# Layer 3: when VectorE normalises and turns the last row tile

## The chip, the cores and the metric

The kernel runs on one core of one Trainium2 chip. The metric is the time of one execution in device microseconds (us). Five engines work side by side, each with its own queue that it runs in order: TensorE (PE; its weight loads are shown as PEld), VectorE (DVE), ScalarE (ACT), GpSimd (POOL) and SyncE (SP), which issues the transfers between the chip's memory (DRAM) and the on-chip memory. Engines wait for one another only where an instruction needs what another has written, or a buffer that another still reads.

## The reference

Four layers run over 2048 rows of 576 numbers: attention, MLP, attention, MLP, each on the layer-normalised rows, each with a residual sum. The attention is linear, with 32 heads of 18.

```python
def _A_ref(x, wqkv, wo):
    B, S, D = x.shape
    H = 32; Dh = D // H
    qkv = (x @ wqkv).reshape(B, S, 3, H, Dh).transpose(2, 0, 3, 1, 4)
    q, k, v = qkv[0], qkv[1], qkv[2]
    phi = lambda t: jnp.where(t > 0, t + 1, jnp.exp(t)) + 1e-6
    pq, pk = phi(q), phi(k)
    kv = jnp.einsum("bhsd,bhse->bhde", pk, v)
    z = jnp.einsum("bhsd->bhd", pk)
    num = jnp.einsum("bhqd,bhde->bhqe", pq, kv)
    den = jnp.einsum("bhqd,bhd->bhq", pq, z)[..., None] + 1e-6
    o = num / den
    return o.transpose(0, 2, 1, 3).reshape(B, S, D) @ wo

x = A_x
x = x + _A_ref(_layernorm(x), A_wqkv, A_wo)
x = x + _B_ref(_layernorm(x), B_w1, B_b1, B_w2, B_b2)   # gelu MLP, 576 -> 4608 -> 576
x = x + _A_ref(_layernorm(x), A_wqkv, A_wo)
x = x + _B_ref(_layernorm(x), B_w1, B_b1, B_w2, B_b2)
```

## The kernel before

**Tiles and names.** The 2048 rows are cut into 16 row tiles t = 0 to 15 of 128 rows, and into 4 blocks c of four tiles. In the code the layers are numbered `li` = 0 to 3, so the third layer is `li` = 2 and of kind "A". `yT` holds the normalised rows turned, with the 576 features along the partitions in five chunks of 128, and the 2048 rows along the free dimension: it is what the projections of queries and keys read.

**From a layer's sum to the next layer's turned rows.** A small state machine (`LNPipe`, from line 342) takes each row tile through the layer norm, one stage per tick: statistics on VectorE (lines 392 to 410), the reciprocal root as a power on GpSimd (line 428), the normalisation into one of three `y_ring` buffers (line 465, on VectorE for the tiles that concern us), and for layer 3 a store of the normalised rows to memory (line 472). One stage later `turn_rows` (line 294) turns 32 x 32 squares of the tile with a VectorE instruction into `turned` (line 297). With the fourth tile of a block, four stores put the turned block into memory (line 305). Three ticks on, `land` loads the block back into its columns of `yT` (lines 320 and 323). For the last block, block 3, it then also loads the last columns of the normalised rows into `v_ring` (line 328) and the rows of tiles 12 to 15 into `yrow_pair` (line 290).

**The last tile.** Tile 15's sum at the end of layer 2 ends that layer's matmuls, so its layer norm runs while layer 3 has already begun. Its statistics carry an order behind a key or query maximum (the `after="phi"` of line 1088, read at line 394); its normalisation and its turning carry none but the data. The places of all instructions on an engine are settled when the program is built, by a scheduler that follows the program's order and such order-only dependencies (`add_manual_dep` with `NOSYNC`).

**The key loop of layer 3** (lines 851 to 862). Step t issues, on TensorE, ten key matmuls in two halves of five (`k_half`, line 645), five query matmuls for one group of heads and one block of 512 rows (`q_proj`, line 614), and five products of the keys and rows of step t - 1 (`rows_by_keys`, line 670). The block 3 of `yT` is read first by the key matmuls of step 12. Each key half and each query tile goes through phi: ScalarE takes the exponential (lines 530 and 547) and, for the first key half and the queries, the value plus one (line 548); VectorE takes a minimum (lines 532 and 553) and a maximum (lines 534 and 555). The second key half takes the value straight from PSUM at line 534, so its PSUM buffer is free only after that maximum. The PSUM pool for these tiles has four buffers, one of which is held throughout the loop by `k2_tail`; the other three go around, so the second key half of step t + 1 needs the buffer of the second key half of step t. `dve_last["phi"]` names the latest maximum issued so far.

**Ticks.** The loop ticks the state machine once per step from step 4 on and a second time from step 7 on. Tile 15 gets its statistics with step 4's tick, its power with step 5's, its normalisation with step 6's and its turning with step 7's first.

**After the loop** come the sums over keys for the other half, the denominators, the output projection with its residual sums (line 598), whose residual rows are loaded at line 574, and layer 4.

Of the kernel before, what the change touches and what calls it, by code (L numbers as in the profile page):

```python
# [16 lines left out]
NT = S // P  # L17
# [17 lines left out]
def build(tc, A_x, A_wqkv, A_wo, B_w1, B_b1, B_w2, B_b2, out, dbg=None, n_layers=4):  # L35
    nc = tc.nc
    dbg = dbg or {}
    with ExitStack() as ctx:
# [112 lines left out]
        NOSYNC = mybir.DependencyInfo(mybir.DependencyClass.NoSync, mybir.DependencyReason.SCHED_ONLY)  # L151
# [22 lines left out]
        def named(name, inst):  # L174
            first_ones[name] = inst
            return inst
# [82 lines left out]
        dve_last = dict(norm=None, sum=None, phi=None)  # L259
# [12 lines left out]
        def first_tail(t, width=65):  # L272

            slot = 2 * (t % 8) + t // 8
            flat = v_ring[slot // 8][:].rearrange("p g c -> p (g c)")
            return flat[:, (slot % 8) * 65:(slot % 8) * 65 + width]
# [17 lines left out]
        def turn_rows(y, t, kind):  # L294

            c, j = divmod(t, TPC)
            turn = nc.vector.transpose(out=turned[:, :, j, :], in_=y[:, 0:D])
            if dve_last["sum"] is not None:
                tc.add_manual_dep(turn.ins, dve_last["sum"], NOSYNC, reason="rows are turned behind the sums")
            if j < TPC - 1:  # L300
                return
            home = y_d[state["turns"] % 2]
            state["turns"] += 1
            for i in range(4):
                store = nc.sync.dma_start(out=home[:, :, i * P:(i + 1) * P].rearrange("j r n -> r j n"),
                                          in_=turned[32 * i:32 * (i + 1), :, :, :].rearrange("r j t c -> r j (t c)"))
            landing.append([3, home, c, kind])
            if kind == "A" and c == NCB - 1:
                sp_last["turned"] = store.ins.name
# [32 lines left out]
        class LNPipe:  # L342
# [11 lines left out]
            def tick(self, transposes=1):  # L354
                land()
                for it in list(self.items):
# [32 lines left out]
                    elif st == 0:  # L389
                        xt = it["xt"]  # L390
                        stt = work.tile([P, 2, 6], F32, name="ln_st", bufs=4)
                        first = nc.vector.bn_stats(out=stt[:, 0, :], in_=xt[:, 0:HALF])
                        second = nc.vector.bn_stats(out=stt[:, 1, :], in_=xt[:, HALF:D])
                        after = dve_last[it["after"]] if it["after"] in ("sum", "phi") else it["after"]
# [34 lines left out]
                    elif st == 2 and it["norm"] != "dve":  # L429
                        nmr = work.tile([P, 1], F32, name="ln_nmr", bufs=4)  # L430
                        nc.gpsimd.tensor_scalar(out=nmr[:], in0=it["mv"][:, 0:1], scalar1=1.0 if it["stats"] == "act" else -1.0,
                                                scalar2=it["rstd"][:, 0:1], op0=ALU.mult, op1=ALU.mult)
                        it["nmr"] = nmr
                    elif st in (2, 3) and it["kind"] == "A" and it["evac"] == "act":
                        xt, t = it["xt"], it["t"]
                        tail = first_tail(t)[:, 0:64]
                        if it["norm"] == "pool":
                            for out, cols in ((xt[:, 0:4 * P], slice(0, 4 * P)), (tail, slice(4 * P, D))):
                                norm = nc.gpsimd.tensor_scalar(out=out, in0=xt[:, cols], scalar1=it["rstd"][:, 0:1],
                                                               scalar2=it["nmr"][:, 0:1], op0=ALU.mult, op1=ALU.add)  # L440
                            pool_last["norm"] = norm.ins.name
                        else:
                            for name, out, cols in ((f"n{t}", xt[:, 0:4 * P], slice(0, 4 * P)), (f"nt{t}", tail, slice(4 * P, D))):
                                norm = named(name, nc.vector.tensor_scalar(
                                    out=out, in0=xt[:, cols], scalar1=it["mv"][:, 0:1], scalar2=it["rstd"][:, 0:1],
                                    op0=ALU.subtract, op1=ALU.mult))
                            dve_last["norm"] = norm.ins.name
                        row_of[t] = xt
                        it["stage"] = 4
                        continue  # L450
                    elif st in (2, 3):
                        if sum(other["stage"] == 4 for other in self.items) == NY:
                            continue
                        y = y_ring[state["ycnt"] % NY]
                        state["ycnt"] += 1
                        xt = it["xt"]
                        if it["norm"] == "act":
                            nc.scalar.activation(out=y[:, 0:D], in_=xt[:, 0:D], func=ACT.Identity,
                                                 scale=it["rstd"][:, 0:1], bias=it["nmr"][:, 0:1])
                        elif it["norm"] == "pool":  # L460
                            norm = nc.gpsimd.tensor_scalar(out=y[:, 0:D], in0=xt[:, 0:D], scalar1=it["rstd"][:, 0:1],
                                                           scalar2=it["nmr"][:, 0:1], op0=ALU.mult, op1=ALU.add)
                            pool_last["norm"] = norm.ins.name
                        else:
                            norm = nc.vector.tensor_scalar(out=y[:, 0:D], in0=xt[:, 0:D], scalar1=it["mv"][:, 0:1],
                                                           scalar2=it["rstd"][:, 0:1], op0=ALU.subtract, op1=ALU.mult)
                            dve_last["norm"] = norm.ins.name
                        if it["kind"] == "B" and it["evac"] != "dma":
                            nc.gpsimd.tensor_copy(out=y[:, D:DPAD], in_=y[:, 4 * P:D])
                        if it["kind"] == "A" and it["evac"] == "dma":  # L470
                            c, j = divmod(it["t"], TPC)
                            nc.sync.dma_start(out=yrow_d[c, :, j], in_=y[:, 0:D])
                        it["y"] = y
                        it["stage"] = 4
                        continue
                    elif st == 4:
                        t = it["t"]
                        first_layer = it["kind"] == "A" and it["evac"] == "act"
                        y = it["xt"] if first_layer else it["y"]
                        if it["evac"] == "dma":  # L480
                            turn_rows(y, t, it["kind"])
                            self.items.remove(it)
                            continue
                        tp = ps_h.tile([P, 512], F32, name="tp", tag="h")
                        tp = tp[:, 0:DPAD // 2].bitcast(BF16).rearrange("p (k n) -> p k n", k=KD)
                        first = first_layer and t < 2
                        tp2 = tp
                        if first:
                            tp2 = ps_h.tile([P, 512], F32, name="tp2", tag="h")
                            tp2 = tp2[:, 0:DPAD // 2].bitcast(BF16).rearrange("p (k n) -> p k n", k=KD)  # L490
                        for k in range(KD):
                            block = first_tail(t, P) if first_layer and k == 4 else y[:, k * P:(k + 1) * P]
                            pe(nc.tensor.transpose(out=(tp if k < 3 else tp2)[:, k, :], in_=block, identity=ident[:]))  # L493
                        if first:
                            named(f"ca{t}", nc.scalar.copy(out=yT[:, 0:3, t * P:(t + 1) * P], in_=tp[:, 0:3, :]))
                            named(f"cd{t}", nc.vector.tensor_copy(out=yT[:, 3:KD, t * P:(t + 1) * P], in_=tp2[:, 3:KD, :]))
                        elif it["evac"] == "act":
                            turned_tile = nc.scalar.copy(out=yT[:, :, t * P:(t + 1) * P], in_=tp)
                            act_last["turned"] = turned_tile.ins.name
                            if first_layer and t < 5:  # L500
                                named(f"ca{t}", turned_tile)
                            elif act_last["exp"] is not None:
                                tc.add_manual_dep(turned_tile.ins, act_last["exp"], NOSYNC, reason="keys go on first")
                        else:
                            nc.vector.tensor_copy(out=yT[:, :, t * P:(t + 1) * P], in_=tp)
                        self.items.remove(it)
                        continue
# [678 lines left out]
```

## Time and profile before

| | |
|---|---|
| median of 3 runs | 762.07 us (761.74 to 762.75) |
| the profiled execution | 762.17 us |
| its span, first to last instruction | 760.5 us |
| granted TensorE clock | 1.000 |
| TensorE busy | 753.6 us |
| VectorE busy | 270.5 us |
| ScalarE busy | 327.9 us |
| GpSimd busy | 117.4 us |

How to read the profile: times are in us from the span's start unless marked ns. A row of the order of time has start, duration, engine, line, operation, tiles as out<-in, shapes and a count; what stands in brackets is the idle time of that engine ahead of the instruction and what ended it. A row of waits has the waiting engine and line, what released it, the total, the number of times and the longest. In the chain that ended last each row has start, duration and what the end waited for in that time. Instructions overlap a little on an engine, so the start of the next one, not the duration, tells how long an instruction holds its queue. The ends of matmuls are modelled.

### The profile page before, as it was taken

The numbers are of one execution on the slowest core, as the hardware profiler recorded it, in microseconds if no ns is written. First come the engines' busy times: TensorE is split into PE (matmuls) and PEld (weight loads), VectorE is DVE, ScalarE is ACT, GpSimd is POOL, SyncE is SP. The second block draws the span as 40 slices with busy tenths as digits, with TensorE's granted clock in tenths as the row PEclk, the third lists the DMA queues.
The fourth block names the chain that finished last, engine by engine and source line by source line (L and its number), as shares of the span: only waits on it lengthen the run. The fifth ranks groups of instructions, "written<-read, shape, count | busy, mean of one in ns | idle before, by whom it ended". The sixth has DMA issues, their size and how long they took to land.

```text
span 760.5 us, 15743 instructions
## 1 busy us (share of the span) xinstructions
PE 753.6 (99%) x6563; PEld 489.4 (64%) x6563; DVE 270.5 (36%) x685; ACT 327.9 (43%) x729; POOL 117.4 (15%) x194
## 2 busy tenths in 40 slices
PE   8999999999999999999999999999999999999998
PEld 5777754774477457646777777447645754674476
DVE  8876862136033503401357577600230132000000
ACT  5886656205700650263056566660164036205600
POOL 4840241002000301200100005300020020001000
PEclk9999999999999999999999999999999999999999
DMA  8994573026312711320304047530240033011000
GB/s 235 266 320 62 169 269 82 17 64 190 82 40 83 179 51 48 112 65 28 120 24 118 18 137 248 191 83 16 79 115 15 16 125 83 9 32 56 1 10 22
DMA packets 80897, 73.82 MB, mean 97 GB/s; under 512 B 36730, under 2 KB 65466, under 8 KB 80826
## 3 DMA queue, kind: packets, MB, share of 16 engines
q1 hardware_dynamic: 80826, 72.82, 32.9%
q8 instruction: 51, 0.84, 0.4%
q14 instruction: 20, 0.16, 0.1%
HBM read 48.03 MB, written 24.77 MB: 96 GB/s over the span
## 4 chain that ended last, share of the span: by engine, by line
PE 95%; DVE 1%; POOL 1%; ACT 1%; DMA 1%; SPq 0%; issue 0%; POOLq 0%; DVEq 0%
PE m_ps L1077 36%; PE h_ps L1019 20%; PE hp_ps L1019 16%; PE q_ps L614 6%; PE k_ps L645 4%; PE wo_ps L907 4%; PE k_ps L670 4%; PE m_half L1077 1%; PE k_tail L670 1%; PE tp L493 1%; DMA x<-in_A_x_dram 1%; PE kv_ps L695 0%; ACT turned L788 0%; PE rden_ps L784 0%; PE den_ps L743 0%
## 5 line engine op out<-in xcount | busy, mean ns | idle before, releaser
L1077 PE MATMUL m_ps<-w_sb,hT 128*128 128x288 bf16 x2232 | 274.8, 286 | 0.0
L1077 PEld LDWEIGHTS <-hT 128*128 128x128 bf16 x2304 | 224.8, 98 | 59.8 <-issue 3.4
L1019 PEld LDWEIGHTS <-w_sb 64*128 64x128 bf16 x2304 | 124.5, 94 | 136.5 <-issue 1.9
L1019 PE MATMUL hp_ps<-yT,w_sb 64*128 64x512 bf16 x1152 | 178.0, 376 | 0.0
L1019 PE MATMUL h_ps<-yT,w_sb 64*128 64x512 bf16 x1152 | 147.9, 376 | 0.0
L1024 ACT COPY relay_sb<-relay_sb 128x1 f32<-128x1 f32 x144 | 28.7, 199 | 259.8 <-PE h_ps L1019 217.5
L1015 ACT ACTIVATE hT<-h_ps,b1T 128x512 bf16<-128x512 f32 x144 | 91.2, 685 | 44.3 <-PE h_ps L1019 44.3
L428 POOL TENSOR_TENSOR ln_rstd<-ln_u,neg_half 128x1 f32<-128x1 f32 x61 | 35.0, 576 | 444.5 <-DVE ln_u L410 219.5
L1015 ACT ACTIVATE hT<-hp_ps,b1T 128x512 bf16<-128x512 f32 x144 | 91.3, 693 | 0.0
L598 DVE TENSOR_TENSOR xbf<-m_ps,xo 128x576 bf16<-128x576 f32 x15 | 11.4, 758 | 213.6 <-PE m_ps L1077 213.6
L598 DVE TENSOR_TENSOR xo<-m_ps,xo 128x576 f32<-128x576 f32 x16 | 12.1, 758 | 174.9 <-PE m_ps L1077 174.9
L581 POOL TENSOR_TENSOR xo<-xo,b_bc 128x576 f32<-128x576 f32 x32 | 41.1, 1288 | 100.8 <-DMA xo<-x_d 62.9
L1019 PE MATMUL h_ps<-yT,w_tail 64*128 64x512 bf16 x144 | 54.1, 376 | 0.0
L1019 PE MATMUL hp_ps<-yT,w_tail 64*128 64x512 bf16 x144 | 54.1, 376 | 0.0
L614 PE MATMUL q_ps<-yT,wqkv_sb 128*126 128x512 bf16 (+1 forms) x200 | 49.3, 379 | 0.1
L645 PE MATMUL k_ps<-wqkv_sb,yT 128*128 128x288 bf16 x320 | 44.8, 286 | 0.9 <-DVE pk L534 0.8
L907 PE MATMUL wo_ps<-kvwo,pq 126*128 126x288 bf16 (+1 forms) x320 | 43.3, 286 | 0.2
L1019 PEld LDWEIGHTS <-w_tail 64*128 64x128 bf16 x288 | 27.1, 94 | 17.1
L645 PEld LDWEIGHTS <-yT 128*128 128x128 bf16 x320 | 31.0, 98 | 9.7 <-issue 1.0
L907 PEld LDWEIGHTS <-pq 126*128 126x128 bf16 (+1 forms) x320 | 30.3, 97 | 8.8 <-issue 0.6
L614 PEld LDWEIGHTS <-wqkv_sb 128*126 128x126 bf16 (+1 forms) x200 | 25.7, 131 | 11.7 <-issue 0.5
L547 ACT ACTIVATE phi_e<-q_ps 126x512 bf16<-126x512 f32 (+1 forms) x40 | 24.0, 599 | 18.4 <-PE q_ps L614 16.7
(131 smaller groups left out, 592.3 us busy)
## 6 DMA issues: line engine op xcount, KB each, us to landing
xo<-x_d SPq DMA_DIRECT2D x48, 288.0 KB, 3.6
x_d<-xo SPq DMA_DIRECT2D x32, 288.0 KB, 2.6
xl<-x_d SPq DMA_DIRECT2D x24, 288.0 KB, 4.3
y_d<-turned SPq DMA_DIRECT2D x40, 144.0 KB, 3.4
w_sb<-in_B_w_dram SPq DMA_DIRECT2D x6, 864.0 KB, 11.0
yT<-y_d SPq DMA_DIRECT2D x10, 512.0 KB, 4.4
w_sb<-in_B_w_dram SPq DMA_DIRECT2D x9, 512.0 KB, 7.7
x_d<-xn SPq DMA_DIRECT2D x16, 288.0 KB, 3.5
```

What stands on the lines that cost most here:

```text
L428: nc.gpsimd.tensor_tensor(out=rstd[:], in0=it["u"][:], in1=neg_half[:], op=ALU.pow)
L547: exp = nc.scalar.activation(out=e_out, in_=ps_ap, func=ACT.Exp)
L581: nc.gpsimd.tensor_tensor(out=xo[:], in0=xo[:], in1=b2_bc[:], op=ALU.add)
L598: total = nc.vector.tensor_tensor(out=xn[:, cols].rearrange("p (h n) -> p h n", h=2), in0=halves, in1=xo[:, cols].rearrange("p (h n) -> p ...
L614: pe(nc.tensor.matmul(qp[0:GR[g], :], lhsT=wqkv_sb[:, k, GO[g]:GO[g] + GR[g]], rhs=yT[:, k, c * CA:(c + 1) * CA], start=(k == 0), stop=(k ...
L645: pe(nc.tensor.matmul(kp[:, 0:HALF], lhsT=yT[:, k, t * P:(t + 1) * P], rhs=wqkv_sb[:, k, D + half * HALF: D + (half + 1) * HALF], start=(k ...
L670: pe(nc.tensor.matmul(dst, lhsT=lhsT, rhs=pk, start=(t == 0), stop=(t == NT - 1)))
L907: pe(nc.tensor.matmul(wp[:, half, 0:HALF], lhsT=pq[(g, c)][0:GR[g], j * P:(j + 1) * P], rhs=kvwo[g][0:GR[g], half * HALF:(half + 1) * HALF ...
L1015: act_last["gelu"] = nc.scalar.activation(out=to, in_=ps, func=ACT.Gelu_apprx_tanh, bias=b1T[:, f:f + 1], scale=1.0).ins.name
L1019: mm = pe(nc.tensor.matmul(dst[n], lhsT=wt, rhs=mv, start=(seen[n] == 0), stop=(seen[n] == 8)))
L1024: relay = nc.scalar.copy(out=relay_sb[:, 1:2], in_=relay_sb[:, 0:1])
L1077: pe(nc.tensor.matmul(acc[half][:, 0:HALF], lhsT=hT[f][:, j * P:(j + 1) * P], rhs=w2_sb[:, f, half * HALF:(half + 1) * HALF], start=(f == ...
```

## The change

Two order-only dependencies are added; no instruction is added, removed or altered. In `turn_rows`, the turning of tile 15 in a layer of kind "A" is put behind the latest maximum issued so far. In the state machine, the normalisation of an item with `after="phi"`, which only tile 15 of layer 2's end has, is put behind the latest maximum too.

```diff
@@ -297,6 +297,8 @@
             turn = nc.vector.transpose(out=turned[:, :, j, :], in_=y[:, 0:D])
             if dve_last["sum"] is not None:
                 tc.add_manual_dep(turn.ins, dve_last["sum"], NOSYNC, reason="rows are turned behind the sums")
+            if kind == "A" and t == NT - 1:
+                tc.add_manual_dep(turn.ins, dve_last["phi"], NOSYNC, reason="keys go on first")
             if j < TPC - 1:
                 return
             home = y_d[state["turns"] % 2]
@@ -464,6 +466,8 @@
                         else:
                             norm = nc.vector.tensor_scalar(out=y[:, 0:D], in0=xt[:, 0:D], scalar1=it["mv"][:, 0:1],
                                                            scalar2=it["rstd"][:, 0:1], op0=ALU.subtract, op1=ALU.mult)
+                            if it["after"] == "phi":
+                                tc.add_manual_dep(norm.ins, dve_last["phi"], NOSYNC, reason="keys go on first")
                             dve_last["norm"] = norm.ins.name
                         if it["kind"] == "B" and it["evac"] != "dma":
                             nc.gpsimd.tensor_copy(out=y[:, D:DPAD], in_=y[:, 4 * P:D])
```

On VectorE the queue around it changes as follows (in the program's order, with the step in brackets): before, key minimum [4], normalisation, key maximum [4], query minimum [4], turning, query maximum [4], then the keys and the query of steps 5, 6 and on. After, the keys and queries of steps 4 and 5 stand first, then the normalisation, then those of step 6, then the turning, then those of step 7. The other engines' instructions keep their order.

## The prediction, made before the changed kernel ran

> **What bounds the kernel now.** I read the page first: TensorE (PE) is busy for nearly the whole span, so only an edit that changes when TensorE stands still can move the time.
>
> ```profile
> span 760.5 us, 15743 instructions
> PE 753.6 (99%) x6563; PEld 489.4 (64%) x6563; DVE 270.5 (36%) x685; ACT 327.9 (43%) x729; POOL 117.4 (15%) x194
> ```
>
> Then I read TensorE's waits from the start of layer 3 (382 us) to the end. There are two, and the larger is the one that the change is about: TensorE waits for `pk`, a key tile that VectorE writes.
>
> ```profile
> PE k_ps L645 <- DVE pk L534: 0.8, 1, 0.8
> PE tp L493 <- POOL y_ring L469: 0.4, 1, 0.4
> ```
>
> The chain that ended last shows what made `pk` late: the normalisation of row tile 15 (line 465) on VectorE, then the key maximum (line 534). Behind it in the chain come the key matmuls of step 5.
>
> ```profile
> 398.19 0.86 DVE y_ring L465
> 399.05 0.37 DVE pk L534
> ```
>
> TensorE's order of time gives the size. A step t of the key loop is ten key matmuls, five query matmuls and the products of the step before. Rows: start, duration, engine.
>
> ```profile
> 394.98 1.39 PE L645 MATMUL k_ps<-wqkv_sb,yT 128*128 128x288 bf16 x10
> ...
> 397.90 0.78 PE L645 MATMUL k_ps<-wqkv_sb,yT 128*128 128x288 bf16 x5
> 399.46 0.77 PE L645 MATMUL k_ps<-wqkv_sb,yT 128*128 128x288 bf16 x5 [0.79 <-DVE pk L534]
> 400.07 1.24 PE L614 MATMUL q_ps<-yT,wqkv_sb 128*126 128x512 bf16 x5
> ...
> 401.76 1.39 PE L645 MATMUL k_ps<-wqkv_sb,yT 128*128 128x288 bf16 x10
> 404.68 1.39 PE L645 MATMUL k_ps<-wqkv_sb,yT 128*128 128x288 bf16 x10
> 407.60 1.39 PE L645 MATMUL k_ps<-wqkv_sb,yT 128*128 128x288 bf16 x10
> 419.26 1.39 PE L645 MATMUL k_ps<-wqkv_sb,yT 128*128 128x288 bf16 x10
> ```
>
> These are steps 4, 5 (in two parts), 6, 7, 8 and 12. Steps 6 to 12 take (419.26 - 401.76) / 6 = 2.92 us each, step 4 takes 397.90 - 394.98 = 2.92, and step 5 takes 401.76 - 397.90 = 3.86. So the stall costs 0.94 us, more than the 0.79 in brackets, which starts only at the modelled end of the matmul before. A second way agrees: five key matmuls advance TensorE by 400.07 - 399.46 = 0.61, so the second half was due at 397.90 + 0.61 = 398.51 and began 0.95 late.
>
> **The change part by part.** No instruction is added or removed. On VectorE two move; TensorE, ScalarE, GpSimd and SyncE keep their order. The two have these neighbours now:
>
> ```profile
> 395.69 0.42 DVE L555 TENSOR_TENSOR pq<-phi_a,phi_e 126x512 bf16<-126x512 bf16 x1 [0.19 <-ACT phi_a L548]
> 396.03 0.45 DVE L392 BATCH_NORM_STATS2 ln_st<-xo 128x6 f32<-128x288 f32 x1
> ...
> 397.37 0.23 DVE L532 TENSOR_SCALAR phi_e<-phi_e 128x288 bf16<-128x288 bf16 x1
> 398.19 0.86 DVE L465 TENSOR_SCALAR y_ring<-xo,ln_mv,ln_rstd 128x576 bf16<-128x576 f32 x1 [0.59 <-POOL ln_rstd L428]
> 398.97 0.44 DVE L534 SCALAR_TENSOR_TENSOR pk<-k_ps,phi_e 128x288 bf16<-128x288 f32 x1
> ...
> 399.58 0.76 DVE L297 STREAM_TRANSPOSE turned<-y_ring 128x576 bf16<-128x576 bf16 x1
> 400.27 0.37 DVE L555 TENSOR_TENSOR pq<-phi_a,phi_e 72x512 bf16<-72x512 bf16 x1
> ...
> 402.52 0.43 DVE L555 TENSOR_TENSOR pq<-phi_a,phi_e 126x512 bf16<-126x512 bf16 x1 [0.25 <-ACT phi_a L548]
> 403.02 0.23 DVE L553 TENSOR_SCALAR phi_e<-phi_e 128x288 bf16<-128x288 bf16 x1
> ...
> 403.63 0.23 DVE L532 TENSOR_SCALAR phi_e<-phi_e 128x288 bf16<-128x288 bf16 x1
> 403.90 0.46 DVE L534 SCALAR_TENSOR_TENSOR pk<-k_ps,phi_e 128x288 bf16<-128x288 f32 x1
> 404.90 0.29 DVE L553 TENSOR_SCALAR phi_e<-phi_e 126x512 bf16<-126x512 bf16 x1 [0.54 <-ACT phi_e L547]
> 405.38 0.43 DVE L555 TENSOR_TENSOR pq<-phi_a,phi_e 126x512 bf16<-126x512 bf16 x1 [0.19 <-ACT phi_a L548]
> 405.94 0.24 DVE L553 TENSOR_SCALAR phi_e<-phi_e 128x288 bf16<-128x288 bf16 x1
> ```
>
> The normalisation goes from in front of the key maximum of step 4 (398.97) to behind the query maximum of step 5 (402.52); the turning goes from in front of the query maximum of step 4 (400.27) to behind that of step 6 (405.38).
>
> *What is taken away.* Without line 465 in between, the key maximum follows its minimum as at 403.63 and 403.90, 0.27 later: 397.37 + 0.27 = 397.64, done at 398.10. TensorE wants it at 398.51. The stall goes with 0.41 us to spare: -0.94 us.
>
> *What the normalisation costs in its new place.* All times behind step 5 come 0.94 earlier, so the query maximum of step 5 starts at 401.58. The next instruction follows such a maximum after 0.34 (395.69 to 396.03): the normalisation starts at 401.92, its inputs long ready, and holds the queue for 398.97 - 398.19 = 0.78, to 402.70. The gap behind the maximum is otherwise 0.56 (405.38 to 405.94), so the next key minimum is late by 0.34 + 0.78 - 0.56 = 0.56. Queued behind it are the key maxima of step 6; the second comes 403.90 - 403.02 = 0.88 after that minimum, at 403.58, done at 404.04. Who waits for it is step 7's second half, due at 404.68 - 0.94 + 0.61 = 404.35. Margin 0.31, cost nothing; VectorE's wait of 0.54 at 404.90 absorbs the delay. Without that cover the price would be at most the whole 0.78.
>
> *The turning* is the same sum: behind the maximum at 405.38 - 0.94 = 404.44 it starts at 404.78 and holds the queue for 400.27 - 399.58 = 0.69. The key minimum behind is late by 0.34 + 0.69 - 0.56 = 0.47, the second key maximum comes at 404.78 + 0.69 + 0.88 = 406.35, done at 406.81, and step 8's second half is due at 407.60 - 0.94 + 0.61 = 407.27. Margin 0.46, cost nothing; at most 0.69.
>
> *What hangs on the two.* SyncE's queue is in order. The store of the normalised rows (line 472) waits for the first, and behind it stand the stores that wait for the second:
>
> ```profile
> 400.37 2.84 SPq L305 DMA_DIRECT2D y_d<-turned  x4
> 405.88 0.38 SPq L320 DMA_DIRECT2D yT<-y_d  x1
> 406.31 0.51 SPq L323 DMA_DIRECT2D yT<-y_d  x1
> 406.92 0.53 SPq L328 DMA_DIRECT2D v_ring<-yrow_d  x1
> 407.50 1.92 SPq L290 DMA_DIRECT2D yrow_pair<-yrow_d  x4
> 409.46 0.43 SPq L574 DMA_DIRECT2D xo<-x_d  x1
> ```
>
> All of them move with the turning, by 404.78 - 399.58 = 5.20 us. The times from issue to landing, for lines 305, 320 and 323 (minimum, median, maximum over the run) and for line 290 in this stretch:
>
> ```profile
> DMA to landing us min/median/max: 2.3/3.4/4.4
> ```
> ```profile
> DMA to landing us min/median/max: 4.2/4.4/5.4
> ```
> ```profile
> DMA to landing us min/median/max: 4.0/4.6/5.3
> ```
> ```profile
> yrow_pair<-yrow_d SPq DMA_DIRECT2D x4, 128.0 KB, 3.5
> ```
>
> The turned rows of tiles 12 to 15 then land at 405.88 + 5.20 + 4.4 = 415.5 and 406.31 + 5.20 + 4.6 = 416.1. Step 12 is the first to read them, at 419.26 - 0.94 = 418.3. Of a slack of 419.26 - 410.9 = 8.4 us now, 2.2 is left. With the longest store (4.4 for 3.4) and the longest load (5.4 for 4.4, 5.3 for 4.6) it is still 0.5. The row loads of line 290 land by 409.4 + 5.2 + 3.5 = 418.1 and are read in step 13, one step after 418.3; line 328 is as small a load and stands ahead of them; the residual row of line 574 waits for the sums behind the loop. Cost nothing.
>
> *What follows.* All later work is released by TensorE, and so shifts whole by 0.94. The only other outside clock would be a transfer, and those are issued behind work that shifts too.
>
> **The sum**, against the profiled execution (762.17 us, of which 760.5 is span): 762.17 - 0.94 + 0 + 0 + 0 = 761.23. That execution stands 0.10 above the median of 762.07, so the median would go to about 761.1; I take 761.2.
>
> One rule bears on the slack. These stores are made of short pieces: in the stretch from 398 to 405.9 us,
>
> ```profile
> DMA packets 2501, 0.75 MB, mean 94 GB/s; under 512 B 2372, under 2 KB 2500, under 8 KB 2500
> ```
>
> The Trainium skill, page "DMA: Bandwidth & Descriptors", section Specifications, says that transfers below 512 B miss line rate, because the engine reads and rewrites. That speaks against handing over these rows late; its cost lies within the 3.4 us already counted, so the sum stays as it is. Only if a second such stream ran at the same time would, as an estimate of mine, the stores take 3.4 us more, 1.2 beyond the slack, and the sum be 762.4.
>
> **The rivals.** (1) *The stall moves one or two steps on.* The margins of 0.31 and 0.46 are smaller than the one removed. For it: VectorE's order is strict, and a signal later than I count by 0.3 us eats the first. Against it: the query minimum at 404.90 waits 0.54 for ScalarE, and that idle time lies where the instructions go. With no margin at all both cost their whole hold: 761.23 + 0.78 + 0.69 = 762.7; with one margin missed by half its hold, 761.6.
>
> (2) *The gain is given back later*, so the change doesn't bring what the stall cost. For it: the end of layer 3 has a chain through GpSimd (the 0.4 us wait above) and two waits for residual rows. Against it:
>
> ```profile
> DVE xo L598 <- DMA xo<-x_d: 1.2, 2, 0.6
> ```
>
> these are waits for loads that are issued behind stores that themselves shift. It gives 762.2.
>
> (3) *Slower: the turned rows come too late for step 12.* Place: the key matmuls at 418.3; price: one for one beyond the slack of 2.2. For it: it is a store to memory and a load back, both 5.20 us later, and three quarters of the slack goes. Against it: the longest landings still leave 0.5. To be slower by 0.2% they must come 2.2 + 0.94 + 1.5 = 4.6 us later than counted; if both hops take twice their median (3.4 and 4.6 more), TensorE waits 8.0 - 2.2 = 5.8 and the time is 767.0.
>
> **How the numbers follow.** What a measurement of this kernel can tell from no change is 0.2%, 1.52 us: 760.55 to 763.59. Forecast 0.72, with 760.5 to 761.8 as its own range (the three runs shown lie from 0.33 below to 0.68 above their median); of this 0.11 falls below 760.55, by the spread alone. Rival 1 0.09, rival 2 0.10, both within 0.2%; rival 3 0.09, mostly above 763.59. So faster 0.11, same 0.80, slower 0.09. The range reaches over rivals 1 and 2 at most of their prices, 760.4 to 762.5.
>
> **What would show it.** In the changed profile: TensorE's waits from 382 us on without `pk`; steps 5, 6 and 7 all at 2.92 us; the normalisation at about 401.9 with no wait for GpSimd ahead of it, the turning at 404.8; the load of line 320 issued near 411.1, and step 12 starting near 418.3 without a wait for `yT`. The forecast is wrong if step 7 or 8 is longer than 2.92 (rival 1), if step 13 starts 0.94 early and the next layer doesn't (rival 2), or if TensorE waits for a transfer at step 12 (rival 3).

## The result, and the profile after

| | kernel before | changed kernel |
|---|---|---|
| median of 21 runs each | 762.05 us (761.45 to 762.81) | 760.74 us (760.51 to 761.26) |
| the profiled execution | 762.17 us | 761.09 us |
| its span | 760.5 us | 759.4 us |

The ratio is 0.9986, with a 95% interval from 0.9979 to 0.9992: the changed kernel is faster by 0.14%, 1.3 us, and the interval goes from 0.6 to 1.6 us. That is inside the 0.2% called "no change" in the prediction, inside its range, and close to its 761.2.

The page of the changed kernel shows the same work in a shorter span, and TensorE's waits from 382 us on have lost the row for `pk`; one wait is left:

```profile
span 759.4 us, 15742 instructions
PE 753.7 (99%) x6563; PEld 489.5 (64%) x6563; DVE 270.3 (36%) x685; ACT 327.6 (43%) x729; POOL 117.3 (15%) x194
```
```profile
PE tp L497 <- POOL y_ring L473: 0.4, 1, 0.4
```

(Lines of the changed kernel are 2 or 4 higher: 465 is 467 now, 534 is 538, 645 is 649, 320 is 322.) TensorE's order of time for steps 4, 5, 6, 7, 8 and 12, each row the ten key matmuls of a step:

```profile
394.85 1.39 PE L649 MATMUL k_ps<-wqkv_sb,yT 128*128 128x288 bf16 x10
...
397.77 1.39 PE L649 MATMUL k_ps<-wqkv_sb,yT 128*128 128x288 bf16 x10
...
400.68 1.39 PE L649 MATMUL k_ps<-wqkv_sb,yT 128*128 128x288 bf16 x10
...
403.60 1.39 PE L649 MATMUL k_ps<-wqkv_sb,yT 128*128 128x288 bf16 x10
...
406.52 1.39 PE L649 MATMUL k_ps<-wqkv_sb,yT 128*128 128x288 bf16 x10
...
418.18 1.39 PE L649 MATMUL k_ps<-wqkv_sb,yT 128*128 128x288 bf16 x10
```

Step 5 is whole again, one row in place of two, and takes 400.68 - 397.77 = 2.91 us; steps 6 and 7 take 2.92 each. Steps 4 and 5 together took 401.76 - 394.98 = 6.78 before and take 400.68 - 394.85 = 5.83 now: 0.95 us. Step 12 starts when TensorE comes to it. VectorE's order of time shows the two in their new places:

```profile
397.24 0.22 DVE L536 TENSOR_SCALAR phi_e<-phi_e 128x288 bf16<-128x288 bf16 x1
397.50 0.46 DVE L538 SCALAR_TENSOR_TENSOR pk<-k_ps,phi_e 128x288 bf16<-128x288 f32 x1
...
401.44 0.43 DVE L559 TENSOR_TENSOR pq<-phi_a,phi_e 126x512 bf16<-126x512 bf16 x1 [0.25 <-ACT phi_a L552]
401.79 0.57 DVE L467 TENSOR_SCALAR y_ring<-xo,ln_mv,ln_rstd 128x576 bf16<-128x576 f32 x1
402.27 0.23 DVE L557 TENSOR_SCALAR phi_e<-phi_e 128x288 bf16<-128x288 bf16 x1
...
403.10 0.46 DVE L538 SCALAR_TENSOR_TENSOR pk<-k_ps,phi_e 128x288 bf16<-128x288 f32 x1
...
404.57 0.42 DVE L559 TENSOR_TENSOR pq<-phi_a,phi_e 126x512 bf16<-126x512 bf16 x1 [0.46 <-ACT phi_a L552]
404.91 0.77 DVE L297 STREAM_TRANSPOSE turned<-y_ring 128x576 bf16<-128x576 bf16 x1
405.61 0.19 DVE L557 TENSOR_SCALAR phi_e<-phi_e 128x288 bf16<-128x288 bf16 x1
...
406.39 0.46 DVE L538 SCALAR_TENSOR_TENSOR pk<-k_ps,phi_e 128x288 bf16<-128x288 f32 x1
```

The key maximum of step 4 follows its minimum by 0.26. The normalisation starts at 401.79 without a wait, and lasts 0.57 where it lasted 0.86 before. SyncE issues the stores and loads of the turned rows so much later:

```profile
405.71 2.46 SPq L307 DMA_DIRECT2D y_d<-turned  x4
410.94 0.38 SPq L322 DMA_DIRECT2D yT<-y_d  x1
411.37 0.51 SPq L325 DMA_DIRECT2D yT<-y_d  x1
```

### The profile page after: what moved, and what is told of

It is laid out like the page before. It is cut to its first block, busy times and chain, and to the rows that moved or that the text cites. A ratio compares the mean times of both kernels' runs of the same rounds, so it can differ in the third digit from the quotient of the medians.

```text
span 759.4 us, 15742 instructions
## 1 busy us (share of the span) xinstructions
PE 753.7 (99%) x6563; PEld 489.5 (64%) x6563; DVE 270.3 (36%) x685; ACT 327.6 (43%) x729; POOL 117.3 (15%) x194
## 4 chain that ended last, share of the span: by engine, by line
PE 97%; POOL 1%; ACT 1%; DVE 1%; issue 0%; POOLq 0%
PE m_ps L1081 36%; PE h_ps L1023 21%; PE hp_ps L1023 16%; PE q_ps L618 6%; PE k_ps L649 5%; PE k_ps L674 4%; PE wo_ps L911 4%; PE m_half L1081 1%; PE k_tail L674 1%; PE tp L497 1%; PE warm_ps L214 1%; PE kv_ps L699 0%; ACT turned L792 0%; PE rden_ps L788 0%; PE den_ps L747 0%; PE kvwo_half L717 0%
```

## The experiments

Two questions stood open: whether the normalisation's place alone made the stall, or both moves share the gain; and how much slack for the turned rows is left. The traces raised a third: why the normalisation was shorter in its new place.

**Each move alone.** In the first kernel the turning's new dependency is taken out of the changed kernel, in the second the normalisation's.

```diff
-            if kind == "A" and t == NT - 1:
-                tc.add_manual_dep(turn.ins, dve_last["phi"], NOSYNC, reason="keys go on first")
...
-                            if it["after"] == "phi":
-                                tc.add_manual_dep(norm.ins, dve_last["phi"], NOSYNC, reason="keys go on first")
```

Expected of the first: 

> Only the normalisation's order is kept; the turning is free again and stands one place behind it, between two key instructions of step 6. Theory (the stall is the place of the normalisation, 0.94 us): no wait of TensorE for pk, step 5 takes 2.92 us, and the time is that of the changed kernel, 760.7. Rival (both moves share the gain): step 5 about 3.4 us and about 761.4.

Expected of the second: 

> Only the turning's order is kept; the normalisation stands where it stood before. Theory: the wait for pk stays at 0.8 us, step 5 takes 3.86 us, and the time is that of the kernel before, 762.0. Rival (both moves share the gain): about 761.4.

Measured: the normalisation alone gives 760.68 us, 0.9984 of before (0.9975 to 0.9993), the whole gain. The turning alone gives 761.94 us, 0.9999 (0.9990 to 1.0007): nothing. TensorE's steps 5 and 6 with the normalisation alone, 400.41 - 397.50 = 2.91 us apart:

```profile
397.50 1.39 PE L647 MATMUL k_ps<-wqkv_sb,yT 128*128 128x288 bf16 x10
...
400.41 1.39 PE L647 MATMUL k_ps<-wqkv_sb,yT 128*128 128x288 bf16 x10
```

The turning reads the normalised rows, so it can't stay where it was; without a dependency of its own it stands just behind the normalisation, with one key minimum in between:

```profile
402.15 0.77 DVE L297 STREAM_TRANSPOSE turned<-y_ring 128x576 bf16<-128x576 bf16 x1
```

And with the turning alone, first TensorE's step 5 in its two parts and step 6, then the two VectorE rows that matter:

```profile
397.48 0.78 PE L647 MATMUL k_ps<-wqkv_sb,yT 128*128 128x288 bf16 x5
399.50 0.77 PE L647 MATMUL k_ps<-wqkv_sb,yT 128*128 128x288 bf16 x5 [1.24 <-DVE pk L536]
...
401.80 1.39 PE L647 MATMUL k_ps<-wqkv_sb,yT 128*128 128x288 bf16 x10
```
```profile
397.77 1.32 DVE L467 TENSOR_SCALAR y_ring<-xo,ln_mv,ln_rstd 128x576 bf16<-128x576 f32 x1 [0.59 <-POOL ln_rstd L430]
399.01 0.44 DVE L536 SCALAR_TENSOR_TENSOR pk<-k_ps,phi_e 128x288 bf16<-128x288 f32 x1
```

So the gain hangs on the normalisation's place: the later turning without it brings nothing, and the turning's own dependency adds nothing to it. But step 5 takes 401.80 - 397.48 = 4.32 here, an excess of 1.40 and not 0.94, because the normalisation, in the same place behind the same wait, lasted 1.32 and not 0.86.

**One place later is not enough.** The third kernel puts the normalisation directly behind the key maximum that it stood in front of, the least move that frees that maximum. `phi_by_dve` keeps a list of its maxima, and the last but one, when the normalisation is issued, is that of step 4. The turning's dependency is taken out. Against the changed kernel (the line that makes the empty list is left out here):

```diff
             dve_last["phi"] = top.ins.name
+            maxima.append(top.ins.name)
...
                             if it["after"] == "phi":
-                                tc.add_manual_dep(norm.ins, dve_last["phi"], NOSYNC, reason="keys go on first")
+                                tc.add_manual_dep(norm.ins, maxima[-2], NOSYNC, reason="keys go on first")
...
-            if kind == "A" and t == NT - 1:
-                tc.add_manual_dep(turn.ins, dve_last["phi"], NOSYNC, reason="keys go on first")
```

Expected: 

> The normalisation is put just one place later, right behind the key maximum of step 4, and the turning stays two places behind it as before. Theory: step 5 takes 2.92 us, but the second key maximum of step 6's predecessor now ends at about 401.48 on the clock of before, against 401.43 when step 6's second half is due, so a stall of about 0.1 us appears in step 6: 760.85. Rival 1 of the prediction (the stall moves on): half of it or more comes back in step 6, 761.3 or slower.

(The sentence says "the second key maximum of step 6's predecessor": that of step 5.) Measured: 761.47 us, 0.9992 of before (0.9983 to 1.0000), 0.7 us above the changed kernel. Step 5 has its 2.92 us, and a stall opens in step 6. TensorE's steps 6 (in two parts) and 7, then VectorE's query minimum of step 4, the turning behind it and the second key maximum of step 5:

```profile
400.28 0.78 PE L650 MATMUL k_ps<-wqkv_sb,yT 128*128 128x288 bf16 x5
401.36 0.77 PE L650 MATMUL k_ps<-wqkv_sb,yT 128*128 128x288 bf16 x5 [0.30 <-DVE pk L538]
...
403.66 1.39 PE L650 MATMUL k_ps<-wqkv_sb,yT 128*128 128x288 bf16 x10
```
```profile
398.43 0.69 DVE L558 TENSOR_SCALAR phi_e<-phi_e 72x512 bf16<-72x512 bf16 x1
399.04 0.76 DVE L297 STREAM_TRANSPOSE turned<-y_ring 128x576 bf16<-128x576 bf16 x1
...
400.84 0.46 DVE L538 SCALAR_TENSOR_TENSOR pk<-k_ps,phi_e 128x288 bf16<-128x288 f32 x1
```

The same query minimum in the kernel before, where the turning followed at 399.58, and the second of GpSimd's three fills in that stretch, in the kernel before and in this one:

```profile
399.33 0.33 DVE L553 TENSOR_SCALAR phi_e<-phi_e 72x512 bf16<-72x512 bf16 x1
```
```profile
398.67 0.84 POOL L622 MEMSET pq<- 32x512 bf16 x1
```
```profile
398.13 0.84 POOL L627 MEMSET pq<- 32x512 bf16 x1
```

Step 6 takes 403.66 - 400.28 = 3.38, an excess of 0.46: rival 1 of the prediction is what happens in this place. The 0.1 expected was too little because the query minimum held the queue for 399.04 - 398.43 = 0.61, where it held it for 0.25 before. A fill ran beside it in both kernels, and in both the minimum ended 0.15 after that fill: at 399.66 against 399.51 before, at 399.12 against 398.97 here. Here it began 0.54 before the end of the fill, and before the change 0.18. The changed kernel's places, behind a query maximum, are therefore part of the gain: there VectorE has idle time to absorb an instruction. One thing isn't separated: in this kernel the turning too stands in front of step 5's keys, and its hold of 0.69 is more than the 0.41 by which the second key maximum of step 5 came late (ended at 401.30, due at 400.28 + 0.61 = 400.89). The normalisation alone in this place, with the turning further back, was not run.

**GpSimd beside the normalisation.** Before the change the normalisation waits for the power on GpSimd, and GpSimd goes straight on to fill the spare rows of query tiles with ones (line 622). Three of its four fills stand there. The fourth kernel is the kernel before with all four at the beginning of the layer, behind the power of tile 14.

```diff
-                    if g == 0 and (first_pq is None or c > 0):
-                        (nc.gpsimd if li > 0 else nc.vector).memset(pq[(g, c)][96:P, 0:CA], 1.0)
+                    if g == 0 and li == 0 and c > 0:
+                        nc.vector.memset(pq[(g, c)][96:P, 0:CA], 1.0)
...
+            ones_pq = {}
+            for c in range(NCA if li > 0 else 0):
+                ones_pq[c] = blk.tile([P, D], BF16, name="pq", tag="blk")
+                ones = nc.gpsimd.memset(ones_pq[c][96:P, 0:CA], 1.0)
+                tc.add_manual_dep(ones.ins, pool_last["power"], NOSYNC, reason="powers first")
```

Expected: 

> The kernel before, with GpSimd's four fills of ones into the query tiles moved from beside the normalisation to the beginning of the layer; VectorE's order is that of before. Theory (the normalisation took 0.86 us there and 0.57 in the changed kernel because a GpSimd fill ran at the same time): it takes 0.58, the stall shrinks by 0.3, step 5 takes about 3.56 us and the time is 761.75. Rival (the 0.86 comes from the wait for the power): still 0.86, step 5 3.86 us, 762.05.

Measured: 761.29 us, 0.9993 of before (0.9984 to 1.0002). The fills, VectorE's normalisation, and TensorE's step 5 (first part) and step 6:

```profile
378.27 2.23 POOL L641 MEMSET pq<- 32x512 bf16 x4
```
```profile
397.82 0.58 DVE L466 TENSOR_SCALAR y_ring<-xo,ln_mv,ln_rstd 128x576 bf16<-128x576 f32 x1 [0.59 <-POOL ln_rstd L428]
```
```profile
397.54 0.78 PE L651 MATMUL k_ps<-wqkv_sb,yT 128*128 128x288 bf16 x5
...
401.12 1.39 PE L651 MATMUL k_ps<-wqkv_sb,yT 128*128 128x288 bf16 x10
```

With the same wait of 0.59 the normalisation now takes 0.58, so the extra time came with the fills and not with the wait. Step 5 takes 401.12 - 397.54 = 3.58, an excess of 0.66, as expected. The time is 0.46 below the 761.75 expected, but the interval holds both.

**Is 1.32 chance or the program?** Five more profiles, three of the kernel before and two of the kernel with the turning alone. 

> The kernel before, unchanged, one more profile. Theory (beside GpSimd's fills the normalisation takes a varying time, 0.86 us in the first profile, 1.32 in the run with the turning alone moved, so that the stall varies too): the normalisation takes between 0.86 and 1.32 or another value above 0.58, and step 5's excess over 2.92 us is that duration less about 0 to 0.1 (0.94 for 0.86, 1.40 for 1.32). Rival: 0.86 and 0.94 again, and the 1.32 belongs to the moved turning.

> The kernel before, unchanged, a third profile: as for the second. Over the three profiles of it the theory expects the mean excess of step 5 nearer 1.3 than 0.94; the rival expects 0.94 each time.

> The kernel with the turning alone moved, a second profile. View 1 (the duration of the normalisation beside GpSimd's fills is a matter of chance in each run, 0.86 or 1.32): either of the two, with 0.94 or 1.40 us of stall in step 5. View 2 (it belongs to the program): 1.32 and 1.40 again.

> The kernel with the turning alone moved, a third profile. View 1: either 0.86 or 1.32 for the normalisation. View 2: 1.32 and a stall of 1.40 us a third time.

> The kernel before, a fourth profile. View 1: either 0.86 or 1.32 for the normalisation beside the fills. View 2: 0.86 and 0.94 us of stall again.

All five show 0.86 and a stall of 0.94 (one of them below). With the first profile of each kernel that is 0.86 six times in seven and 1.32 once, in a kernel that showed 0.86 twice afterwards: the program doesn't settle it. (The 1.32 was seen on one chip and the two later profiles were taken on another, so what part the chip has stays open.) The expectation for the second and third profile of the kernel before, a mean nearer 1.3, failed: over the seven the mean excess is 0.94 + 0.46 / 7 = 1.0 us.

```profile
398.55 0.86 DVE L465 TENSOR_SCALAR y_ring<-xo,ln_mv,ln_rstd 128x576 bf16<-128x576 f32 x1 [0.59 <-POOL ln_rstd L428]
```

The fills show what the two durations are. Here are the first of the three in the first profile of the kernel before, and the second in the profile that showed 1.32:

```profile
398.21 0.52 POOL L622 MEMSET pq<- 32x512 bf16 x1
```
```profile
398.25 0.52 POOL L624 MEMSET pq<- 32x512 bf16 x1
```

In the first the normalisation ended at 399.05, 0.32 after the end of the first fill (398.73); so it does in the other five, to within 0.01. In the second it ended at 399.09, 0.32 after the end of the second fill (398.77). It behaves as if it had waited for one fill in six profiles and for two in one; the fills start 0.46 apart, which is the difference of 1.32 and 0.86. Why a second fill went ahead of it in that one is not shown.

**How much later may the rows be turned?** In the fifth and sixth kernel the normalisation of the changed kernel sits out three and five more ticks (the number 3 below is 5 in the sixth); the turning follows one tick behind it.

```diff
                     elif st in (2, 3):
+                        if it["after"] == "phi" and it.setdefault("skip", 3) > 0:
+                            it["skip"] -= 1
+                            continue
```

Expected: 

> The changed kernel with normalisation and turning held back by three more ticks: the turning stands behind the first key maximum of step 8, about 3.7 us later than in the changed kernel (404.9 there). Theory (rival 3 of the prediction: beyond the slack one pays one for one): the first load of turned rows is issued at about 414.6 and lands at 419.0, the second at 419.7, while step 12 wants the first at 418.18 and the second 0.49 later: TensorE waits about 1.0 us for the load at step 12 and the time is 761.7. Other view (the loads have more slack than counted): no wait, 760.7.

> Five more ticks: the turning stands behind the first key maximum of step 9, 2.9 us later still. Theory: TensorE waits 1.0 + 2.9 = 3.9 us for the load at step 12, 764.6. Other view: the wait grows by less than the delay because the transfers meet less traffic, 763 to 764.

Measured, three ticks: 761.72 us, 0.9996 of before (0.9986 to 1.0006). The first load of the turned rows, then steps 11 and 12 of TensorE:

```profile
414.52 0.38 SPq L322 DMA_DIRECT2D yT<-y_d  x1
```
```profile
414.98 1.39 PE L652 MATMUL k_ps<-wqkv_sb,yT 128*128 128x288 bf16 x10
...
418.78 1.40 PE L652 MATMUL k_ps<-wqkv_sb,yT 128*128 128x288 bf16 x10 [0.72 <-DMA yT<-y_d]
```

Step 12 was due at 414.98 + 2.92 = 417.90 and is 0.88 late, 4.26 after the load was issued; about 1.0 was expected. The whole gain but 0.25 is gone. Five ticks: 767.62 us, 1.0074 (1.0059 to 1.0089), the median of four runs and 3.0 more than expected. Its load, and its steps 11, 12 and 13:

```profile
418.47 0.38 SPq L322 DMA_DIRECT2D yT<-y_d  x1
```
```profile
415.67 1.39 PE L652 MATMUL k_ps<-wqkv_sb,yT 128*128 128x288 bf16 x10
...
422.87 2.58 PE L652 MATMUL k_ps<-wqkv_sb,yT 128*128 128x288 bf16 x10 [4.13 <-DMA yT<-y_d]
...
427.42 1.39 PE L652 MATMUL k_ps<-wqkv_sb,yT 128*128 128x288 bf16 x10
```

Step 12 is 422.87 - (415.67 + 2.92) = 4.28 late, which is 3.40 more than with three ticks. Measured from the start of step 11 the load was issued 3.26 later (418.47 - 415.67 = 2.80, against 414.52 - 414.98 = -0.46), and it landed 0.14 later after its issue (4.40 for 4.26): one for one. Step 12 then takes 427.42 - 422.87 = 4.55 in place of 2.92. The reason stands in the rows of the granted clock (the stretch and its length, busy time and count of instructions of PE, PEld, DVE, ACT and POOL in it, then the clock, the share of the DMA engines and GB/s):

```profile
422.00:423.00 1.00, 0.13 (x1) 0.13 (x2) 0.00 (x0) 0.00 (x0) 0.00 (x0) 0.90 1.11 215
423.00:424.00 1.00, 1.00 (x5) 0.61 (x5) 0.00 (x0) 0.00 (x0) 0.00 (x0) 0.50 1.06 309
424.00:425.00 1.00, 1.00 (x6) 0.61 (x4) 0.23 (x1) 0.71 (x2) 0.00 (x0) 0.50 0.94 332
425.00:426.00 1.00, 1.00 (x4) 0.69 (x3) 0.37 (x2) 0.42 (x2) 0.00 (x0) 0.50 0.09 32
426.00:427.00 1.00, 1.00 (x6) 0.61 (x5) 0.63 (x2) 0.00 (x0) 0.00 (x0) 0.90 0.00 0
```

After more than 4 us of standing still TensorE worked at half its clock for over 3 us, 1.63 us lost on top of the wait. The Trainium skill, page "TensorE: Matmul & The Clock Gate", Part 1, says that the clock is halved after an idle window of about 3.4 us and comes back after a busy one; this run agrees. After the stall of 0.88 us in the fifth kernel the clock stayed at 1.00. The two parts explain the profiled executions: 767.41 here and 761.09 for the changed kernel differ by 6.32, which is 4.28 + 1.63 and 0.40 by which step 4 starts later (395.25 and 394.85). The medians differ by 1.0 more than 4.28 + 1.63; a start of step 4 that varies between executions can carry part of that, which is not shown.

## Why the prediction was right

*The stall and its price.* The term of -0.94 us for the normalisation in front of the key maximum is what the profiles show: 6.78 us for steps 4 and 5 before, 5.83 after. The first two experiments show that this move brings it, and the turning's dependency none of it. The key maximum of step 4 ends at 397.96 and is due at 397.77 + 0.61 = 398.38: a margin of 0.42 for the 0.41 predicted.

*The cost in the new places.* A cost of nothing was predicted, and there is none, but the margins came out otherwise than worked out. The second key maximum of step 6 ends at 403.56 and is due at 403.60 + 0.61 = 404.21, a margin of 0.65 for 0.31 predicted, mostly because the normalisation holds the queue for 0.48 and not 0.78: its price was taken from a row in which it ran beside GpSimd's fills. That of step 7 ends at 406.85, due at 407.13, a margin of 0.28 for 0.46, because VectorE stood idle for 0.46 ahead of the query maximum in front of the turning, where 0.19 had been read. The profile puts that wait down to ScalarE, whose value plus one ended at 403.68 + 0.59 = 404.27; the maximum began only at 404.57, and what held it for the last 0.30 is open. So the forecast of no cost held here by less than it counted on, and partly by luck: one more such delay would have used the margin up.

*The turned rows.* The forecast of 411.08 for the first load was 410.94, and of 418.3 for step 12 it was 418.18. The slack of 2.2 was set by the median landing of the second load, 4.6 us. In the fifth kernel TensorE resumed 4.26 after the first load's issue and ran its ten matmuls in 1.40 us, without a second wait; by that measure the slack in the changed kernel is 418.18 - (410.94 + 4.26) = 3.0.

*The later stages.* Rival 2 is out: from the start of step 6 to the end of the span it was 760.5 - 401.76 = 358.74 before and is 759.4 - 400.68 = 358.72.

*The size.* The medians differ by 1.3 us, the stall by 0.95 in the profiles. The interval holds both. The two profiled executions differ by 762.17 - 761.09 = 1.08, which is the 0.95 and 0.13 by which step 4 starts earlier in the changed kernel (394.98 and 394.85). Two things in the runs can carry the rest, neither shown to: the longer normalisation beside the fills, seen in one profile of seven, and the time before step 4, which the change doesn't touch: in the four profiles of the kernel before, step 4 starts anywhere from 394.55 to 395.35. The part above 0.95 stays open.

## What to carry to other kernels

On an in-order engine that feeds the bottleneck, work that isn't urgent belongs behind the last urgent instruction of a period, where the engine has idle time, and not merely behind the one that it delayed: one place later, with the turning close behind, gave back about half of the gain. Before moving such work, follow what it feeds to its first reader: here the loads were issued 5.06 us later and about 3 us of slack were left; beyond that the loss was one for one at first, and more once TensorE stood still for 4 us. A duration read from a profile includes the company that the instruction had there; moved, it can be another.

## What the runs showed of the hardware that was not expected

A VectorE normalisation of 128x576 from f32 to bf16 takes 0.58 us alone; beside GpSimd's fills of 32x512 it took 0.86 in six profiles and 1.32 in one, at the same place behind the same wait, and each time it ended about 0.32 after the end of a fill: of the first in the six, of the second in the one. The Trainium skill, page "GPSIMD Engine Reference", section Specifications, says that GpSimd shares its SBUF interfaces with VectorE and names the instructions that contend; it gives no price, and the fourth experiment's 0.86 to 0.58 is one. The price was not the same in three profiles of one program.
